# Sums of four rows of q, k and v for the late head pairs: one VectorE instruction each in place of two GpSimd additions

## The chip, the cores and the metric

The kernel runs on one core of a Trainium2 chip. Five engines have instruction queues of their own and work through them in order: TensorE (PE, its weight loads shown apart as PEld), VectorE (DVE), ScalarE (ACT), GpSimd (POOL) and SyncE (SP), which here issues all DMAs. Semaphores order them against each other. The metric is the device time of one execution in microseconds (us); lower is better.

## The reference

Attention for 8 batches and 8 heads, sequence 576, head size 64, in two parts that are added: a global attention on q, k and v averaged over groups of four rows, and a local one with a band of seven keys. A feed-forward network follows.

```python
def _attn_ref(q, k, v):
    q_d = q.reshape(B, H, Sd, factor, D).mean(axis=3)      # factor = 4
    k_d = k.reshape(B, H, Sd, factor, D).mean(axis=3)
    v_d = v.reshape(B, H, Sd, factor, D).mean(axis=3)
    out_up = np.repeat(sm_attn(q_d, k_d, v_d), factor, axis=2)
    mask = np.abs(pos[:, None] - pos[None, :]) < factor
    ...
    return (out_up + out_local).astype(np.float32)

def _moe_ref(x, U, V, w_ch1, w_ch2):
    xt = x.transpose(0, 2, 1)
    h = xt @ U @ V
    u = x + h.transpose(0, 2, 1)
    ch = np.maximum(u @ w_ch1, 0.0) @ w_ch2
    return (u + ch).astype(np.float32)
```

## The kernel before

**Attention** goes by pairs of heads, 32 in all, four to a batch. The four pairs of batch 0 are "early" (`early_global`, `local_blocks`, `early_mix`); the 28 others are "late" and go through `late_global` (L515), `local_attn` (L817) and `mix_part` (L899).

A late pair loads q and k transposed (tiles `gq` and `gT`, 128 partitions, L587) and, for each head, v as `vr` (72 partitions, L528). `pool_halves` (L437) sums each four neighbours of `gq` and of `gT` on GpSimd in two additions: L440 makes `gh`, L442 makes `smq` or `smk`. The v sums are two GpSimd additions for each head: L530 in place, L532 into `vs`. TensorE then makes the scores (`ps_b`, L783 and L790), later transposes the exponentials (`ps_t`, L555) and multiplies by `vs` (`ps_a`, L569). The tiles `gq`, `gT`, `gh` and `vr` have one buffer each, so the next load into one waits until its readers are done.

The local part of a pair keeps GpSimd busy with five products `Pt` (L852), which VectorE reduces (L857), and with `xL` (L923). The mix makes `ps_hu` (L931), `stk` (ScalarE L935 and L939, VectorE L936), `ps_u` (L739), the sum `xT` (VectorE L743), and from it `uH` (ScalarE L746) and `uL` (GpSimd L748), the input of the network.

**The network** runs over 13 tiles of columns (four of 288, nine of 384) times 16 slices of the weights: 208 steps. A step is twelve matmuls into a PSUM tile `ps_h` (`ffn1`, L956), which ScalarE reads into `hH` (L964) and VectorE into `hL` (L965), and three steps later twelve matmuls into `acc` (`ffn2`, L981). Up to step 19 only one bank serves `ps_h`, since the conversion of the weights uses the other; from then on two banks alternate (L950). Tiles 0 and 1 hold batch 0. Tiles 2 and 3 hold batch 1, so step 33 can't run before the four late pairs of batch 1 are through the mix. This point is called the gate below.

**The weights** are loaded (`wr`) and converted during the first steps: ScalarE L347, VectorE L350 and L352, ScalarE L358, GpSimd L362.

**The order** of each engine's queue is made ahead of the run by a planner (`Plan`, L55): every operation has an engine, an estimated duration, a priority, and its dependencies; the planner runs the whole program by these estimates, and an engine that is free takes the ready operation of the best priority. `dve(n, ...)` puts an operation of n elements on VectorE, `pool_tt(n, ...)` on GpSimd. A different engine or duration for a few operations thus orders all queues anew.

Of the kernel before, what the change touches and what calls it, by code (L numbers as in the profile page):

```python
# [11 lines left out]
F32 = mybir.dt.float32  # L12
# [7 lines left out]
ALU = mybir.AluOpType  # L20
AX = mybir.AxisListType
# [33 lines left out]
class Plan:  # L55
# [6 lines left out]
    def buf(self, pool, shape, dt, name, tag=None, bufs=1):  # L62
        return Buf(self, pool, shape, dt, name, tag or name, bufs)

    def op(self, eng, dur, fn, r=(), w=(), prio=0.0, after=(), lat=None, move=0.0, at=0.0, hold=0.0):
        o = Op()
        o.eng, o.dur, o.fn, o.prio, o.succ, o.ndep, o.ready = eng, dur, fn, prio, [], 0, at
        o.lat, o.move = LATENCY[eng] + SLACK * (SLACK_FROM <= prio < 1000) if lat is None else lat, move
        deps = set(after)
        deps.update(d for k in (*r, *w) for d in getattr(getattr(k[0] if isinstance(k, tuple) else k, "pool", None), "gate", ()))  # L70
        bufs = []
        for k in r:
            b = k[0] if isinstance(k, tuple) else k
# [130 lines left out]
def attn_mix_ffn_kernel(ctx: ExitStack, tc, q, kp, vp, qT, kT, v, U, Ub, V, w1, w2, band, eye, pool, vw, ident, outT):  # L204
    nc = tc.nc
    B, H, S, D = q.shape
    HP = H // 2
    NPOS = 9
    SPAD = kp.shape[2]
    SD = S // 4  # L210
# [38 lines left out]
    op, buf = plan.op, plan.buf  # L249
# [23 lines left out]
    def dve(n, fn, r, w, prio, two_x=False, after=()):  # L273
        return op(DVE, ((n / 2 if two_x else n) + 65) / 960.0, fn, r, w, prio, after)
# [4 lines left out]
    def pool_tt(n, fn, r, w, prio, ns=2.11, after=()):  # L279
        return op(POOL, 0.147 + n * ns / 1000.0, fn, r, w, prio, after)  # L280
# [8 lines left out]
    early_pool = early.__enter__()  # L289
# [11 lines left out]
    loc, glo, mix = (Late(n) for n in ("loc", "glo", "mix"))  # L301
# [129 lines left out]
    def work(is_early, pool, shape, dt, name, tag=None, bufs=1):  # L431
        if is_early:
            return buf(early_pool, shape, dt, name, tag, 1 if name == 'gh' else 2)
        return buf(pool, shape, dt, name, tag, bufs)

    heads = [slice(hh * D, (hh + 1) * D) for hh in range(2)]
    def pool_halves(raw, lo, out, e, prio):  # L437
        gh = work(e, glo, [128, SD, 2], F32, "gh")
        x4 = lambda: raw()[:, lo:lo + S].rearrange("p (j r) -> p j r", r=4)
        pool_tt(2 * SD, lambda: nc.gpsimd.tensor_tensor(  # L440
            out=gh(), in0=x4()[..., 0:2], in1=x4()[..., 2:4], op=ALU.add), [raw], [gh], prio, 1.65)
        pool_tt(SD, lambda: nc.gpsimd.tensor_tensor(  # L442
            out=out()[:, 0:SD], in0=gh()[..., 0], in1=gh()[..., 1], op=ALU.add), [gh], [out], prio, 1.75)

    def early_global(b, hp, prio, qt, kt):
        sq = ring([SD + 16], "smq_e")
        sk = work(True, glo, [128, SD], F32, "smk")
        pool_halves(qt, 0, sq, True, prio)
        pool_halves(kt, (SPAD - S) // 2, sk, True, prio)
        od = buf(early_pool, [128, NQ, D], F32, "od_e", None, NOD)  # L450
        vs = buf(early_pool, [QH, 4 * D], F32, "vs_e", None, 2)
        x = (buf(early_pool, [QH, 2, 2, 4, D], F32, "vr") if b else
             buf(wts, [QH, 2, 2, 4, D], F32, "vr", f"W2_{NFC - 6 - hp}:vr"))
        for hh in range(2):
            dma(lambda hh=hh: nc.sync.dma_start(
                out=x()[:, hh], in_=v[b, 2 * hp + hh].rearrange("(a p r) d -> p a r d", a=2, r=4)), [], [(x, hh)], prio, 150)
        pool_tt(512, lambda: nc.gpsimd.tensor_tensor(
            out=x()[:, :, :, 0:2, :], in0=x()[:, :, :, 0:2, :], in1=x()[:, :, :, 2:4, :], op=ALU.add),
            [(x, 0), (x, 1)], [(x, 0), (x, 1)], prio)
        pool_tt(256, lambda: nc.gpsimd.tensor_tensor(  # L460
            out=vs()[:QH].rearrange("p (a h d) -> p h a d", a=2, h=2), in0=x()[:, :, :, 0, :], in1=x()[:, :, :, 1, :],
            op=ALU.add), [(x, 0), (x, 1)], [vs], prio)
# [7 lines left out]
        def s_mm():  # L470
# [8 lines left out]
            out=mx(), in_=pooled_view(ps), axis=AX.X, op=ALU.max), [ps], [mx], prio)  # L479
# [20 lines left out]
        out = lambda: pa()[:, :NQ * D].rearrange("p (a d) -> p a d", a=NQ)  # L500

        def a_mm():
# [8 lines left out]
            out=od()[:NP], in0=out()[:NP], in1=ri()[:NP].unsqueeze(2).broadcast_to([NP, NQ, D]), op=ALU.mult),  # L511
# [3 lines left out]
    def late_global(b, hp, up_s, prio):  # L515
        h0 = 2 * hp
        g = lambda shape, name, bufs=1: buf(glo, shape, F32, name, None, bufs)
        sq, sk = queries[0], g([128, SD], "smk")
        qr, kr = g([128, S], "gq"), g([128, SPAD], "gT")
        load_t(qr, qT, b, h0, prio)  # L520
        load_t(kr, kT, b, h0, prio)
        pool_halves(qr, 0, sq, False, prio)
        pool_halves(kr, (SPAD - S) // 2, sk, False, prio)
        vss = []
        for hh in range(2):
            x, vs = g([QH, 2, 4, D], "vr"), g([QH, 2, D], "vs", 2)
            vss.append(vs)
            dma(lambda hh=hh, x=x: nc.sync.dma_start(  # L528
                out=x(), in_=v[b, h0 + hh].rearrange("(a p r) d -> p a r d", a=2, r=4)), [], [x], prio, 150)
            pool_tt(256, lambda x=x: nc.gpsimd.tensor_tensor(  # L530
                out=x()[:, :, 0:2, :], in0=x()[:, :, 0:2, :], in1=x()[:, :, 2:4, :], op=ALU.add), [x], [x], prio)
            pool_tt(128, lambda x=x, vs=vs: nc.gpsimd.tensor_tensor(  # L532
                out=vs(), in0=x()[:, :, 0, :], in1=x()[:, :, 1, :], op=ALU.add), [x], [vs], prio)
        s_s = buf(dram, [2, S, KL + 1], F32, "s_s", bufs=4)
        ps = late_scores(qr, kr, sq, sk, s_s, prio - 0.4)
        rs, rr, ri, mx, nb = (g([128, NQ], n) for n in ("rs", "rr", "ri", "mx", "nb"))
# [4 lines left out]
            out=mx(), in_=pooled_view(ps), axis=AX.X, op=ALU.max), [ps], [mx], prio)  # L541
# [20 lines left out]
        out = lambda: pa()[:, :NQ * D].rearrange("p (a d) -> p a d", a=NQ)  # L562

        def a_mm():
# [9 lines left out]
            out=od()[:NP], in0=out()[:NP], in1=ri()[:NP].unsqueeze(2).broadcast_to([NP, NQ, D]), op=ALU.mult),  # L574
# [11 lines left out]
    def load_t(t, src, b, h0, prio):  # L586
        dma(lambda: nc.sync.dma_start(out=t(), in_=src[b, h0:h0 + 2].rearrange("h d s -> (h d) s")),  # L587
            [], [t], prio)
# [274 lines left out]
    for g0 in (*range(0, NB * S, TN), *range(NB * S, B * S, TW)):  # L863
        n = TN if g0 < NB * S else TW
        for b in range(g0 // S, (g0 + n - 1) // S + 1):
            lo, hi = max(g0, b * S), min(g0 + n, (b + 1) * S)
# [237 lines left out]
```

## Time and profile before

| what | value |
|---|---|
| median of 3 runs | 1010.79 us (1009.43 to 1011.28) |
| the profiled execution's own time | 1003.93 us |
| its span, first to last instruction | 1002.2 us |
| mean granted TensorE clock in it | 0.986 |
| first of the late sums on GpSimd | 68.2 us after the start |
| last of them (L530) | 750.0 us after the start |

In the profile, a group row gives the line, the engine, the operation, the tiles (written<-read), the shapes, the count, then the busy time in us and the mean of one in ns, and last the engine's idle time just before these instructions with what ended it. A window row gives the busy time of each engine in one stretch of the span, the granted clock (1.00 is full), the share of the DMA engines, and GB/s. A timeline row gives start, duration, and in brackets the idle time before it with its releaser. A row of waits gives total, times, and the longest in us.

### The profile page before, as it was taken

The numbers are of one execution on the slowest core, as the hardware profiler recorded it, in microseconds if no ns is written. First come the engines' busy times: TensorE is split into PE (matmuls) and PEld (weight loads), VectorE is DVE, ScalarE is ACT, GpSimd is POOL, SyncE is SP. The second block draws the span as 40 slices with busy tenths as digits, with TensorE's granted clock in tenths as the row PEclk, the third lists the DMA queues.
The fourth block names the chain that finished last, engine by engine and source line by source line (L and its number), as shares of the span: only waits on it lengthen the run. The fifth ranks groups of instructions, "written<-read, shape, count | busy, mean of one in ns | idle before, by whom it ended". The sixth has DMA issues, their size and how long they took to land.

```text
span 1002.2 us, 24561 instructions
## 1 busy us (share of the span) xinstructions
PE 976.2 (97%) x9896; PEld 942.6 (94%) x9896; DVE 438.3 (44%) x814; ACT 347.1 (35%) x1012; POOL 571.7 (57%) x640
## 2 busy tenths in 40 slices
PE   6979999999999999999999999999999999999998
PEld 4669999899999999999999999999999999999998
DVE  4776664645544454544543544434445222211211
ACT  4866533433333333333433333423422122111110
POOL 6786887986757587657846756844866212300100
PEclk9969999999999999999999999999999999999999
DMA  9958768665554565547545456355462121000000
GB/s 265 317 186 210 205 154 155 154 162 137 131 121 111 130 167 130 132 105 179 144 116 128 102 137 144 83 127 113 113 150 72 32 56 24 32 2 1 32 1 32
DMA packets 220906, 120.04 MB, mean 120 GB/s; under 512 B 174052, under 2 KB 196920, under 8 KB 220792
## 3 DMA queue, kind: packets, MB, share of 16 engines
q1 hardware_dynamic: 220792, 118.47, 47.7%
q8 instruction: 78, 1.28, 0.6%
q14 instruction: 36, 0.29, 0.1%
HBM read 87.57 MB, written 30.86 MB: 118 GB/s over the span
## 4 chain that ended last, share of the span: by engine, by line
PE 86%; DMA 2%; POOL 1%; DVE 1%; ACT 1%; SPq 1%; issue 0%; DVEq 0%; ACTq 0%
PE ps_h L956 38%; PE acc L981 38%; PE ps_a L569 2%; PE ps_b L790 2%; DMA wr<-in_W 2%; PE ps_b L783 2%; PE ps_t L555 2%; PE ps_hu L931 2%; POOL Pt L852 1%; PE ps_u L739 1%; DMA vr<-in_v 1%; SPq L806 1%; DVE acc L857 0%; ACT half L347 0%; ACT E L544 0%
## 5 line engine op out<-in xcount | busy, mean ns | idle before, releaser
L981 PE MATMUL acc<-hH,W 128*128 128x384 f32 (+1 forms) x1664 | 442.3, 327 | 0.0
L956 PE MATMUL ps_h<-uH,W 128*128 128x384 f32 (+1 forms) x1376 | 360.4, 323 | 3.9 <-DVE hL L965 2.9
L981 PEld LDWEIGHTS acc<-hH,W 128*128 128x128 f32 x1664 | 297.3, 188 | 2.4
L981 PE MATMUL acc<-hL,W 128*128 128x384 f32 (+1 forms) x832 | 268.0, 322 | 0.0
L852 POOL TENSOR_TENSOR Pt<-vl,ms 128x896 f32<-128x896 f32 (+1 forms) x140 | 239.6, 1790 | 28.4 <-DMA vl<-in_vp 14.0
L956 PEld LDWEIGHTS ps_h<-uH,W 128*128 128x128 f32 x1376 | 246.3, 190 | 5.7 <-DVE hL L965 3.5
L965 DVE SCALAR_TENSOR_TENSOR hL<-ps_h,hH 128x384 fp32r<-128x384 f32 (+1 forms) x208 | 108.9, 524 | 324.1 <-ACT hH L964 323.8
L964 ACT ACTIVATE hH<-ps_h 128x384 fp32r<-128x384 f32 (+1 forms) x208 | 97.3, 468 | 366.8 <-PE ps_h L956 358.9
L956 PE MATMUL ps_h<-uL,W 128*128 128x384 f32 (+1 forms) x688 | 221.7, 322 | 1.1 <-POOL uL L748 1.1
L857 DVE TENSOR_REDUCE acc<-Pt 128x128 f32<-128x1024 f32 (+1 forms) x140 | 152.8, 1108 | 62.3 <-ACT Pt L846 27.1
L981 PEld LDWEIGHTS acc<-hL,W 128*128 128x128 f32 x832 | 156.7, 188 | 0.0
L956 PEld LDWEIGHTS ps_h<-uL,W 128*128 128x128 f32 x688 | 130.6, 190 | 1.7 <-POOL uL L748 1.7
L956 PE MATMUL ps_h<-u,W 128*128 128x384 f32 x432 | 98.1, 334 | 0.0
L923 POOL TENSOR_TENSOR xL<-xL,xH 116x640 fp32r<-116x640 f32 x28 | 43.9, 1567 | 73.4 <-ACT xH L922 66.8
L846 ACT ACTIVATE Pt<-ul 128x128 f32<-128x128 f32 (+1 forms) x140 | 56.6, 433 | 81.7 <-DVE acc L857 54.9
L991 POOL TENSOR_TENSOR o<-uH,uL 128x384 f32<-128x384 f32 (+1 forms) x43 | 39.0, 940 | 70.0 <-DMA out_t<-o 70.0
L956 PEld LDWEIGHTS ps_h<-u,W 128*128 128x128 f32 x432 | 76.9, 188 | 0.0
L748 POOL TENSOR_TENSOR uL<-xT,uH 128x384 fp32r<-128x384 f32 (+2 forms) x52 | 41.0, 808 | 56.7 <-ACT uH L746 56.7
L530 POOL TENSOR_TENSOR vr<-vr 72x256 f32<-72x256 f32 x56 | 41.2, 736 | 52.4 <-DMA vr<-in_v 51.7
L362 POOL TENSOR_TENSOR W<-c,W 128x512 fp32r<-128x512 f32 x32 | 41.0, 1289 | 14.3 <-ACT W L358 14.3
L743 DVE TENSOR_TENSOR xT<-ps_u,xT 128x384 f32<-128x384 f32 (+2 forms) x64 | 27.4, 452 | 37.2 <-PE ps_u L739 37.1
L790 PE MATMUL ps_b<-smk,smq 64*32 64x144 f32 x672 | 38.9, 296 | 0.0
(133 smaller groups left out, 897.2 us busy)
## 6 DMA issues: line engine op xcount, KB each, us to landing
wr<-in_W SPq DMA_DIRECT2D x32, 511.8 KB
vl<-in_vp SPq DMA_DIRECT2D x56, 240.0 KB
vr<-in_v SPq DMA_DIRECT2D x64, 144.0 KB
gT<-in_kT SPq DMA_DIRECT2D x28, 291.0 KB
gq<-in_qT SPq DMA_DIRECT2D x28, 288.0 KB
up_s<-od SPq DMA_DIRECT2D x168, 48.0 KB
ul<-up_s SPq DMA_DIRECT2D x28, 288.0 KB
x_s<-acc SPq DMA_DIRECT2D x28, 288.0 KB
```

Source lines behind the costliest of these rows:

```text
L362: pool_tt(1.0 * n, lambda: nc.gpsimd.tensor_tensor(out=lo_out(), in0=ta()[l0:], in1=hi_out()[l0:].bitcast(F32), op=ALU.subtract), [t, *own ...
L530: pool_tt(256, lambda x=x: nc.gpsimd.tensor_tensor(out=x()[:, :, 0:2, :], in0=x()[:, :, 0:2, :], in1=x()[:, :, 2:4, :], op=ALU.add), [x], ...
L748: pool_tt(n, lambda uH=uH, uL=uL, uf=uf, us=us: nc.gpsimd.tensor_tensor(out=uL.ap(hp, us), in0=uf(), in1=uH.ap(hp, us).bitcast(F32), op=AL ...
L790: nc.tensor.matmul(pg()[m:m + QL, a * SD:(a + 1) * SD], sq()[o, n:n + QL], sk()[o], start=True, stop=True)
L846: act(n * D, lambda n=n, ps=ps, Pt=Pt: nc.scalar.activation(Pt()[:, :n, :, 7], ul()[:, ps, :], AF.Copy), [ul], [(Pt, 1)], prio, 0.16)
L852: nc.gpsimd.tensor_tensor(out=Pt()[:, :n, :, 0:7].rearrange("p s d o -> p o s d"), in0=win, in1=at()[:, ps, :].rearrange("p s o -> p o s") ...
L857: dve(8.5 * n * D, lambda n=n, ps=ps, Pt=Pt: nc.vector.tensor_reduce(out=acc()[:, ps, :], in_=Pt()[:, :n], axis=AX.X, op=ALU.add), [(Pt, 0 ...
L923: pool_tt(640, lambda: nc.gpsimd.tensor_tensor(out=xL(), in0=xL().bitcast(F32), in1=xH().bitcast(F32), op=ALU.subtract), [xL, xH], [xL], prio)
L956: nc.tensor.matmul(ps()[:, :tn], W1[fc]()[:, w, dc, :], u.ap(dc), start=(n == 0), stop=(n == 3 * NDC - 1))
L964: last_h[i] = act(tn, lambda: nc.scalar.activation(hH()[:, :tn], ps()[:, :tn], AF.Relu), [ps], [hH], FIRST, 0.05)
L965: dve(tn, lambda: nc.vector.scalar_tensor_tensor(hL()[:, :tn], ps()[:, :tn], 0.0, hH()[:, :tn].bitcast(F32), op0=ALU.max, op1=ALU.subtract ...
L981: nc.tensor.matmul(ac[e]()[:, :tn], W2[fc]()[:, w, es], hx()[:, :tn], start=(fc == 0 and n == 0), stop=(fc == NFC - 1 and n == 2))
```

## The change

The late pairs get `pool_late`: one VectorE `tensor_reduce` over groups of four for `smq`, one for `smk`, and one for each head's `vs`, which reads the four rows of v that stand 64 elements apart. The eight GpSimd additions of a late pair and its buffer `gh` go. The early pairs keep `pool_halves`.

```diff
+    def pool_late(raw, lo, out, prio):
+        dve(S, lambda: nc.vector.tensor_reduce(
+            out=out()[:, 0:SD], in_=raw()[:, lo:lo + S].rearrange("p (j r) -> p j r", r=4), axis=AX.X, op=ALU.add),
+            [raw], [out], prio)
+
-    def pool_halves(raw, lo, out, e, prio):
-        gh = work(e, glo, [128, SD, 2], F32, "gh")
+    def pool_halves(raw, lo, out, prio):
+        gh = work(True, early_pool, [128, SD, 2], F32, "gh")
...
-        pool_halves(qr, 0, sq, False, prio)
-        pool_halves(kr, (SPAD - S) // 2, sk, False, prio)
+        pool_late(qr, 0, sq, prio)
+        pool_late(kr, (SPAD - S) // 2, sk, prio)
...
-            pool_tt(256, lambda x=x: nc.gpsimd.tensor_tensor(
-                out=x()[:, :, 0:2, :], in0=x()[:, :, 0:2, :], in1=x()[:, :, 2:4, :], op=ALU.add), [x], [x], prio)
-            pool_tt(128, lambda x=x, vs=vs: nc.gpsimd.tensor_tensor(
-                out=vs(), in0=x()[:, :, 0, :], in1=x()[:, :, 1, :], op=ALU.add), [x], [vs], prio)
+            dve(512, lambda x=x, vs=vs: nc.vector.tensor_reduce(
+                out=vs(), in_=x().rearrange("p a r d -> p a d r"), axis=AX.X, op=ALU.add), [x], [vs], prio)
```

From L438 on, lines of the changed kernel stand three to five numbers higher: L965 becomes L968, L748 becomes L751, L852 becomes L855, L835 becomes L838.

VectorE's queue around the first `hL` of the network, before (`y_h`, `c` and `cu` belong to the conversion of weights, `Ust` to that of U):

```order
L352 SCALAR_TENSOR_TENSOR cu<-ur,y_h 116x160
L350 TENSOR_SCALAR y_h<-half 128x512
L366 SCALAR_TENSOR_TENSOR Ust<-cu,Ust 116x5x32
L352 SCALAR_TENSOR_TENSOR c_1267<-wr,y_h 128x512
L965 SCALAR_TENSOR_TENSOR hL<-ps_h,hH 128x288
```

The same place in the changed kernel:

```order
L352 SCALAR_TENSOR_TENSOR cu<-ur,y_h 116x160
L350 TENSOR_SCALAR y_h<-half 128x512
L438 TENSOR_REDUCE smq<-gq 128x144
L438 TENSOR_REDUCE smk<-gT 128x144
L968 SCALAR_TENSOR_TENSOR hL<-ps_h,hH 128x288
L535 TENSOR_REDUCE vs<-vr 72x128
L366 SCALAR_TENSOR_TENSOR Ust<-cu,Ust 116x5x32
L352 SCALAR_TENSOR_TENSOR c_1267<-wr,y_h 128x512
```

The sums of the first late pair stand ahead of the first `hL`, and two operations of the conversion have moved behind it.

VectorE's queue between the 13th and the 15th `hL`, before (`lsm` and `lrl` belong to the local softmax, `mx` to the global one):

```order
L965 SCALAR_TENSOR_TENSOR hL<-ps_h,hH 128x288
L352 SCALAR_TENSOR_TENSOR c_2043<-wr,y_h 128x512
L965 SCALAR_TENSOR_TENSOR hL<-ps_h,hH 128x288
L831 TENSOR_REDUCE lsm<-ms 128x9
L540 TENSOR_REDUCE mx<-ps_b 128x3
L833 RECIPROCAL lrl<-lse 128x9
L965 SCALAR_TENSOR_TENSOR hL<-ps_h,hH 128x288
```

And in the changed kernel:

```order
L968 SCALAR_TENSOR_TENSOR hL<-ps_h,hH 128x288
L350 TENSOR_SCALAR y_h<-half 128x512
L552 RECIPROCAL ri<-rr 128x3
L834 TENSOR_REDUCE lsm<-ms 128x9
L352 SCALAR_TENSOR_TENSOR c_2168<-wr,y_h 128x512
L968 SCALAR_TENSOR_TENSOR hL<-ps_h,hH 128x288
L535 TENSOR_REDUCE vs<-vr 72x128
L836 RECIPROCAL lrl<-lse 128x9
L438 TENSOR_REDUCE smq<-gq 128x144
L968 SCALAR_TENSOR_TENSOR hL<-ps_h,hH 128x288
```

A sum of v, which waits for a load, and a sum of q, which waits for another, stand between two `hL`, the second of them directly ahead of one.

GpSimd's queue ahead of the gate, before, from the last `xL` of batch 1 to its `uL`:

```order
L923 TENSOR_TENSOR xL<-xL,xH 116x640
L852 TENSOR_TENSOR Pt<-vl,ms 128x7x128 x2
L852 TENSOR_TENSOR Pt<-vl,ms 128x7x64
L826 TENSOR_TENSOR ms<-sc,lmx 128x63
L440 TENSOR_TENSOR gh<-gq 128x288
L530 TENSOR_TENSOR vr<-vr 72x2x128
L442 TENSOR_TENSOR smq<-gh 128x144
L532 TENSOR_TENSOR vs<-vr 72x128
L748 TENSOR_TENSOR uL<-xT,uH 128x288 x2
L835 TENSOR_TENSOR ms<-ms,lrl 128x63
```

In the changed kernel:

```order
L926 TENSOR_TENSOR xL<-xL,xH 116x640
L829 TENSOR_TENSOR ms<-sc,lmx 128x63
L838 TENSOR_TENSOR ms<-ms,lrl 128x63
L855 TENSOR_TENSOR Pt<-vl,ms 128x7x128 x2
L751 TENSOR_TENSOR uL<-xT,uH 128x288 x2
L926 TENSOR_TENSOR xL<-xL,xH 116x640
```

The four sums and one `Pt` are gone from in front of `uL`, and the second `ms`, which waits for VectorE's `lrl`, with two whole `Pt` behind it, now stands ahead of `uL`, where before it stood behind. On TensorE the transposes `ps_t` of a later pair (L558) now stand between `ps_u` and the gate's first `ps_h`; before, none did. On VectorE the last operations ahead of the gate's `stk` are now the fourth read of `acc` (L997), `ri` (L552) and `lrl` (L836).

More of the change, by code (lines that the diff above doesn't have):

```diff
@@ L447, in early_global @@
         sk = work(True, glo, [128, SD], F32, "smk")
-        pool_halves(qt, 0, sq, True, prio)
-        pool_halves(kt, (SPAD - S) // 2, sk, True, prio)
+        pool_halves(qt, 0, sq, prio)
+        pool_halves(kt, (SPAD - S) // 2, sk, prio)
         od = buf(early_pool, [128, NQ, D], F32, "od_e", None, NOD)
```

## The prediction

> **What bounds the kernel now.** I read the page's totals first, then the windows, then the group rows that price the change.
>
> ```profile
> span 1002.2 us, 24561 instructions
> PE 976.2 (97%) x9896; PEld 942.6 (94%) x9896; DVE 438.3 (44%) x814; ACT 347.1 (35%) x1012; POOL 571.7 (57%) x640
> PE 86%; DMA 2%; POOL 1%; DVE 1%; ACT 1%; SPq 1%; issue 0%; DVEq 0%; ACTq 0%
> ```
>
> TensorE is busy 97% of the span, and the chain that ended last runs through it for 86%. GpSimd, from which work is taken, holds 1% of the chain. So GpSimd's time matters only where TensorE waits, and the windows show where that is:
>
> ```profile
> 68.90:139.50 70.60, 68.41 (x805) 66.20 (x806) 44.62 (x82) 37.90 (x99) 56.97 (x66) 0.97 0.75 199
> 150.00:200.00 50.00, 48.45 (x602) 47.03 (x600) 27.68 (x53) 20.90 (x66) 42.73 (x48) 1.00 0.72 154
> 200.00:250.00 50.00, 48.38 (x651) 46.50 (x650) 25.18 (x49) 18.35 (x61) 37.21 (x41) 0.97 0.63 148
> 250.00:300.00 50.00, 50.00 (x509) 49.24 (x508) 23.75 (x45) 18.77 (x57) 32.57 (x39) 1.00 0.56 128
> 550.00:600.00 50.00, 49.31 (x421) 47.57 (x420) 24.21 (x43) 16.48 (x50) 33.62 (x39) 1.00 0.52 118
> ```
>
> The columns behind the stretch are the busy times of PE, PEld, DVE, ACT and POOL. From 250 us on TensorE hardly stops (50.00 of 50); 550 to 600 lacks 0.69. Idle TensorE under the late pairs is 2.2 us in the first 19 steps (68.9 to 139.5), 1.55 and 1.62 on both sides of the gate near 200, and the clock dips there (0.97 of 50 us, 1.5 us). All that GpSimd could give back is some 7 us, and most of it has other causes too.
>
> **What goes from GpSimd.**
>
> ```profile
> L530 POOL TENSOR_TENSOR vr<-vr 72x256 f32<-72x256 f32 x56 | 41.2, 736 | 52.4 <-DMA vr<-in_v 51.7 <-PE ps_h L956 0.7
> L532 POOL TENSOR_TENSOR vs<-vr 72x128 f32<-72x128 f32 x56 | 25.8, 460 | 1.6
> L440 POOL TENSOR_TENSOR gh<-gq 128x288 f32<-128x288 f32 x28 | 18.9, 675 | 12.2 <-DMA gq<-in_qT 12.2
> L440 POOL TENSOR_TENSOR gh<-gT 128x288 f32<-128x288 f32 x28 | 18.7, 669 | 7.0 <-DMA gT<-in_kT 5.6
> L442 POOL TENSOR_TENSOR smk<-gh 128x144 f32<-128x144 f32 x32 | 13.7, 427 | 1.5
> L442 POOL TENSOR_TENSOR smq<-gh 128x144 f32<-128x144 f32 x28 | 11.9, 426 | 1.6
> ```
>
> A late pair loses 0.675 + 0.669 + 0.427 + 0.426 + 2 x (0.736 + 0.460) = 4.59 us; 28 pairs 128.5 us, GpSimd falls from 572 to 443.
>
> **What comes to VectorE.** No row has a sum over groups of four, so I go by the nearest reductions, and for the stride by the nearest pair of strided and dense rows:
>
> ```profile
> L857 DVE TENSOR_REDUCE acc<-Pt 128x128 f32<-128x1024 f32 x112 | 134.8, 1216 | 60.7 <-ACT Pt L846 27.1 <-POOL Pt L852 25.1 <-issue 4.4
> L857 DVE TENSOR_REDUCE acc<-Pt 128x64 f32<-128x512 f32 x28 | 18.9, 674 | 1.6 <-POOL Pt L852 1.5
> L846 ACT ACTIVATE Pt<-ul 128x128 f32<-128x128 f32 x112 | 47.2, 458 | 59.7 <-DVE acc L857 33.0 <-DMA ul<-up_s 25.6 <-POOL xL L923 0.8
> L846 ACT ACTIVATE Pt<-ul 128x64 f32<-128x64 f32 x28 | 9.3, 333 | 22.0 <-DVE acc L857 21.9
> L746 ACT ACTIVATE uH<-xT 128x384 fp32r<-128x384 f32 x18 | 8.6, 518 | 9.9 <-PE ps_h L956 9.6 <-DVE xT L743 0.4
> L746 ACT ACTIVATE uH<-xT 128x192 fp32r<-128x192 f32 x18 | 6.0, 358 | 7.6 <-PE ps_h L956 3.2 <-DVE xT L743 3.2 <-POOL o L991 1.3
> ```
>
> From 1216 and 674 ns a reduction costs (1216 - 674)/512 = 1.06 ns for each element read and 132 ns besides: 0.742 us for 576 dense elements of q or k, 0.674 us for 512. But v is read in steps of 64 elements. ScalarE's strided write (L846, steps of 8 elements) costs (458 - 333)/64 = 1.95 ns an element, its dense one (L746) (518 - 358)/192 = 0.83. If VectorE's strided read pays the same 1.12 ns on top, a sum of v takes 0.674 + 512 x 0.00112 = 1.25 us. I take 1.25, the one strided row of a streaming engine that I have, and keep 0.674 as the other end. VectorE gains 28 x 2 x 0.742 + 56 x 1.25 = 111.5 us (79 at the low end), from 438 to 550 or 518. That still fits the span.
>
> The Trainium skill ("SBUF — State Buffer", section "Door 1: The DMA port swizzle") says that full bandwidth needs consecutive accesses to hit the same 16-byte line, and that every crossing to a new line pays. Steps of 64 fp32 cross each time, so by it the sums of v cost 70 us rather than 38; it gives no factor.
>
> **Term 1, the first 19 steps: +3.8 us.** Here one `ps_h` bank serves, so the next step's twelve matmuls wait for `hL`.
>
> ```profile
> L965 DVE SCALAR_TENSOR_TENSOR hL<-ps_h,hH 128x288 fp32r<-128x288 f32 x64 | 29.0, 453 | 45.9 <-ACT hH L964 45.7
> L964 ACT ACTIVATE hH<-ps_h 128x288 fp32r<-128x288 f32 x64 | 26.3, 411 | 58.8 <-PE ps_h L956 58.5
> 138.77 1.58 PE acc L981 x12
> ```
>
> The cover is the 1.58 us of `acc` matmuls; `hH` and `hL` use 0.41 + 0.45 of it, so 0.72 is left. The new order puts 15 sums between the 1st and the 19th `hL`, eight of q and k and seven of v: 10.7 to 14.7 us more in a stretch where VectorE works 44.6 of 70.6, so 78% to 84% busy. All may fit its 26 us of idle time (0 lost), or each may push TensorE by its length (14.7). Item by item: two sums of v and two of q or k stand directly ahead of an `hL`; beyond the cover that is 2 x (1.25 - 0.72) + 2 x 0.02 = 1.1. And VectorE takes over the waits for the loads:
>
> ```profile
> POOL vr L530 <- DMA vr<-in_v: 2.5, 2, 1.5
> POOL gh L440 <- DMA gq<-in_qT: 1.6, 1, 1.6
> ```
>
> These rows are of GpSimd's waits in 68.9:139.5; three waits of 4.1 us less three covers leave 2.0. That makes 3.1. By scaling instead: the 2.2 us lost now, at a ratio of VectorE's busy to idle time of 44.6/26.0 = 1.7, would grow to 6.7 at 59.3/11.3 = 5.2, so +4.5. I take 3.8, between the two.
>
> **Term 2, the gate: -0.7 us.** The timelines of GpSimd and TensorE there, a group row of VectorE, and a row of the chain:
>
> ```profile
> 181.37 3.89 POOL L852 TENSOR_TENSOR Pt<-vl,ms 128x896 f32<-128x896 f32 x2 [0.39 <-DMA vl<-in_vp]
> 201.37 1.55 POOL L748 TENSOR_TENSOR uL<-xT,uH 128x288 fp32r<-128x288 f32 x2
> 202.88 0.29 POOL L835 TENSOR_TENSOR ms<-ms,lrl 128x63 f32<-128x63 f32 x1
> 196.19 0.46 PE L931 MATMUL ps_hu<-xH,Ust 116*64 116x128 f32 x5
> 198.50 0.50 PE L739 MATMUL ps_u<-Vst,stk 128*128 128x288 f32 x2 [1.55 <-DVE stk L936]
> 201.22 0.40 PE L956 MATMUL ps_h<-uH,W 128*128 128x288 f32 x1 [1.03 <-ACT uH L746]
> 202.21 0.41 PE L956 MATMUL ps_h<-uL,W 128*128 128x288 f32 x1 [0.59 <-POOL uL L748]
> L994 DVE SCALAR_TENSOR_TENSOR o<-acc,o 128x288 f32<-128x288 f32 x16 | 6.5, 454 | 0.3 <-PE acc L981 0.2
> 625.71 0.66 PE ps_t L555 x6
> ```
>
> TensorE waits 1.55 + 1.03 + 0.59 = 3.2 us here, and `uL` lets it go 6.0 us after `ps_hu` began (196.19 to 202.2). In the new order the four sums and a `Pt` are out of the way, but two whole `Pt` (3.89) and a `ms` that waits for VectorE's `lrl` stand ahead of `uL`. `lrl` comes behind the last read of `acc`, which ends with the matmuls just ahead of `ps_hu`; I put it 0.9 us behind the start of `ps_hu` (that read, 0.45, and two short reciprocals; an estimate). Then 0.3 for `ms`, 3.9 for `Pt`, 0.8 (half of 1.55) for the first `uL`: 5.9 us, as late as now. What improves is that the transposes of a later pair (0.66) fill part of the wait. Ends: all of 3.2 and the dip of 1.5 gained (-4.7), or `lrl` 2 us later (+1.5).
>
> **Term 3, the stop in 550 to 600: -0.7 us.** Its chain went through a `vr` load that waited for the GpSimd sum of the head before. One VectorE instruction frees `vr` sooner; at most the 0.69 goes.
>
> **Term 4, waits for loads from step 20 on: +1.1 us.**
>
> ```profile
> POOL vr L530 <- DMA vr<-in_v: 51.7, 21, 9.7
> POOL gh L440 <- DMA gq<-in_qT: 12.2, 7, 3.3
> POOL gh L440 <- DMA gT<-in_kT: 5.6, 3, 2.4
> L965 DVE SCALAR_TENSOR_TENSOR hL<-ps_h,hH 128x384 fp32r<-128x384 f32 x144 | 79.9, 555 | 278.2 <-ACT hH L964 278.1
> L964 ACT ACTIVATE hH<-ps_h 128x384 fp32r<-128x384 f32 x144 | 70.9, 493 | 308.0 <-PE ps_h L956 300.4 <-PE ps_u L739 7.4
> 640.02 2.08 PE ps_h L956 x12
> ```
>
> These 69.5 us move to VectorE, and `hL` queues behind. With two banks the cover is three groups of twelve matmuls, 3 x 2.08 = 6.2, less `hH` 0.49 and `hL` 0.56: 5.2 us. Of 31 waits one, of 9.7, is longer, and would cost 4.5. Between 0 and 4.5, or more if such waits multiply, I take a quarter.
>
> Sum: 3.8 - 0.7 - 0.7 + 1.1 = +3.5 on the profiled execution's 1003.93 us, so 1007.4. The three timed runs lie higher (median 1010.79); the same 3.5 on it gives 1014.3.
>
> **Rivals.** *The relief wins, faster*: VectorE's 26 us of idle time hide the sums in the early steps (term 1 zero), no long wait lands on it (term 4 zero), and `uL` runs ahead of the two `Pt` in effect, because `lrl` comes before `acc` ends. Then 3.2 at the gate and 0.7 in 550 to 600 go: 1006.9, and 1005.4 with the clock dip gone too. For it speaks GpSimd's 42.73 of 50 us ahead of the gate; against it, that `uH` and `stk`, of other engines, ended most of the gate's wait. It decides whether the stretch to step 19 keeps its 2.2 us of idle TensorE. The Trainium skill ("GPSIMD Engine Reference", section "4.1 Engine selection") sends elementwise work and reductions along the free dimension to VectorE, GpSimd being about half as fast; taken as a rule for this kernel it means this case. Here 4.59 us a pair become 2.83 to 3.98 by the rows above, so the trace agrees on the work, not on what TensorE waits for.
>
> *Hidden anyway, no change*: the losses fit the cover and the gate stays as it is: 1010.8. For it speaks 50.00 of 50 in the stretch from 250 us.
>
> *Long waits on VectorE, much slower*: with loads issued in a new order, two more waits like that of 9.7 us stand ahead of an `hL`: 3.5 + 2 x 4.5 = +12.5, 1023. It needs waits beyond 5.2 us; before there was one.
>
> **How the numbers follow.** Forecast case 0.45 (from +1 to +8; 0.38 slower, 0.07 the same), relief 0.23 (0.20 faster, 0.03 the same), hidden 0.20, long waits 0.12. About 0.2%, 2 us, is what a measurement of this kernel can tell from no change. Faster 0.20, same 0.30, slower 0.50. The range from 1006 to 1022 leaves out the end of the relief case with the dip gone (0.06) and the worse half of the long waits (0.06), and holds both prices of a sum of v. The likeliest case's own range is 1011.8 to 1019.
>
> **What would show it.** The sums of q and k as VectorE rows near 0.74 us, those of v near 1.25 rather than 0.67; GpSimd at 443 us. Term 1: TensorE's idle time from the first to the 19th `hL` near 6 us, with waits of `ps_h` for `hL`. Term 2: waits of about 2.5 us at the gate, the last ended by `uL`. Term 4: VectorE waits for `gq`, `gT` and `vr`, few beyond 5 us. I am wrong if the early steps lose nothing, if the gate opens before GpSimd's two `Pt` are done, or if TensorE stops after 250 us.

## The result and the profile after

The changed kernel takes 1016.79 us (median of 9 runs, 1012.54 to 1020.71), the kernel before 1010.79 us in the same session (9 runs, 1008.22 to 1012.53). The ratio is 1.0071, 95% interval 1.0049 to 1.0092: slower by 0.7%. The profiled execution took 1016.65 us.

The totals and the chain on the page of the changed kernel:

```profile
span 1014.9 us, 24387 instructions
PE 977.7 (96%) x9896; PEld 941.9 (93%) x9896; DVE 520.9 (51%) x926; ACT 344.6 (34%) x1012; POOL 454.9 (45%) x416
PE 68%; DMA 8%; DVE 7%; SPq 4%; POOL 3%; issue 2%; ACT 2%; DVEq 0%; ACTq 0%; POOLq 0%
```

GpSimd has lost 117 us of work and VectorE has gained 83. TensorE does the same 9896 matmuls, but the chain that ended last now runs through it for 68% instead of 86%; DMA and VectorE hold 15% of it, 3% before. So work now ends late on other engines. The windows show where. The first row of the next fence runs from the first `hL` to the 19th, the stretch of the prediction's first row; the others are single stretches of 50 us and all that lies behind 250 us. The columns are as before (PE, PEld, DVE, ACT, POOL, granted clock, DMA share, GB/s):

```profile
72.60:143.50 70.90, 70.21 (x902) 67.77 (x903) 57.59 (x103) 39.32 (x110) 43.55 (x36) 0.95 0.85 215
200.00:250.00 50.00, 46.02 (x557) 43.64 (x556) 30.89 (x58) 18.12 (x59) 26.35 (x22) 1.00 0.66 156
400.00:450.00 50.00, 47.76 (x501) 45.89 (x500) 31.81 (x53) 16.96 (x52) 31.08 (x26) 1.00 0.58 133
500.00:550.00 50.00, 47.97 (x489) 46.05 (x495) 33.61 (x54) 16.42 (x53) 24.28 (x20) 0.97 0.62 151
550.00:600.00 50.00, 48.47 (x588) 46.02 (x589) 31.53 (x53) 19.77 (x65) 27.66 (x26) 1.00 0.64 153
250.00:1014.90 764.90, 753.67 (x6648) 736.61 (x6646) 345.94 (x597) 216.15 (x639) 297.46 (x258) 1.00 0.40 93
```

The first 19 steps, where the prediction put most of the loss, lost nothing: TensorE is idle for 70.90 - 70.21 = 0.7 us (2.2 before) although VectorE is busy for 81% of that stretch. Just ahead of it one of the sums does stop TensorE, for 1.88 us:

```profile
72.86 0.46 PE L793 MATMUL ps_b<-smk,smq 64*32 64x144 f32 x4 [1.88 <-DVE smk L438]
```

But from the first step of the network to the 19th `hL`, that stop included, TensorE is idle for 4.0 us where it was 4.5 before. And the 33rd `hL`, the first behind the gate, starts 140.1 us after the first step in both profiles. So up to the gate nothing was lost. From 250 us to the end TensorE is idle for 11.2 us. The kernel before, in the same view:

```profile
250.00:1002.20 752.20, 747.79 (x6628) 732.96 (x6626) 287.73 (x519) 218.66 (x640) 378.03 (x413) 1.00 0.40 95
```

There it was 4.4. In both, 3.7 us of this lie behind TensorE's last matmul, so that the stops are 7.5 us after and 0.7 before. The difference, 6.8 us, is made of single stops in a stretch that hardly had any.

The two profiled executions are 12.7 us apart, the medians 6.0. Part of that is not the change: the first step of the network starts at 63.2 us in the profile of before and at 67.0 in that of after, while the queues up to there differ in nothing. From the first step on the two profiles differ by 8.8 us. The profile of before is also that of a short execution, 1003.93 us, where the nine timed ones begin at 1008.22. So the two profiles show more loss than the medians do.

**One of the new stops.** Timeline rows of ScalarE, VectorE and TensorE of the changed kernel, out of the stretch from 538 us on:

```profile
538.32 0.45 ACT L849 ACTIVATE Pt<-ul 128x128 f32<-128x128 f32 x1 [5.08 <-DMA ul<-up_s]
...
538.85 1.22 DVE L860 TENSOR_REDUCE acc<-Pt 128x128 f32<-128x1024 f32 x1 [7.26 <-ACT Pt L849]
...
540.45 1.21 DVE L860 TENSOR_REDUCE acc<-Pt 128x128 f32<-128x1024 f32 x1
541.58 1.07 DVE L535 TENSOR_REDUCE vs<-vr 72x128 f32<-72x512 f32 x1
...
542.70 1.09 PE L572 MATMUL ps_a<-vs,E 72*48 72x64 f32 x22 [2.03 <-DVE vs L535]
```

Read it from the bottom. TensorE stops for 2.03 us because `ps_a` needs a sum of v. The sum stands in VectorE's queue behind the local reductions `acc` of another pair. The first of these had VectorE stand idle for 7.26 us, since ScalarE's `Pt` waited 5.08 us for `ul`, which had to come back from DRAM. A load that lands late thus stops TensorE through whatever stands behind it in an in-order queue.

**The prices.** Group rows of VectorE after, with its waits for the loads of the sums:

```profile
L535 DVE TENSOR_REDUCE vs<-vr 72x128 f32<-72x512 f32 x56 | 60.9, 1087 | 28.7 <-DMA vr<-in_v 28.6
L438 DVE TENSOR_REDUCE smk<-gT 128x144 f32<-128x576 f32 x28 | 20.8, 743 | 8.7 <-DMA gT<-in_kT 8.7
L438 DVE TENSOR_REDUCE smq<-gq 128x144 f32<-128x576 f32 x28 | 20.7, 738 | 13.5 <-DMA gq<-in_qT 13.4
L860 DVE TENSOR_REDUCE acc<-Pt 128x64 f32<-128x512 f32 x28 | 18.8, 673 | 2.3 <-POOL Pt L855 1.8 <-ACT Pt L849 0.3
```

A sum of q or k takes 0.74 us, as worked out. A sum of v takes 1.087 us, between the two ends of 0.674 and 1.25; the last row, as many elements without the stride, takes 0.673, so the stride of 64 elements costs (1087 - 673)/512 = 0.81 ns an element. (A v sum also writes 128 results where that row writes 64. The sums of q and k write 144 and still cost what the dense rows gave, so the number of results isn't what costs.) VectorE waits 28.6 + 8.7 + 13.4 = 50.7 us for the loads of the sums.

### The profile page after: what moved, and what is told of

Same layout as the page of the kernel before. It is cut to its first block, busy times and chain, and to the rows that moved or that the text cites. A ratio compares the mean times of both kernels' runs of the same rounds, so it can differ in the third digit from the quotient of the medians.

```text
span 1014.9 us, 24387 instructions
## 1 busy us (share of the span) xinstructions
PE 977.7 (96%) x9896; PEld 941.9 (93%) x9896; DVE 520.9 (51%) x926; ACT 344.6 (34%) x1012; POOL 454.9 (45%) x416
## 4 chain that ended last, share of the span: by engine, by line
PE 68%; DMA 8%; DVE 7%; SPq 4%; POOL 3%; issue 2%; ACT 2%; DVEq 0%; ACTq 0%; POOLq 0%
PE acc L984 30%; PE ps_h L959 30%; DVE acc L860 3%; DMA ul<-up_s 3%; POOL Pt L855 2%; SPq L582 2%; PE ps_a L572 2%; DMA vr<-in_v 1%; PE ps_b L793 1%; DMA wr<-in_W 1%; PE ps_hu L934 1%; PE ps_b L786 1%; PE ps_t L558 1%; SPq L809 1%; DMA x_s<-acc 1%
## 5 line engine op out<-in xcount | busy, mean ns | idle before, releaser
L855 POOL TENSOR_TENSOR Pt<-vl,ms 128x896 f32<-128x896 f32 (+1 forms) x140 | 241.4, 1790 | 96.0 <-DVE acc L860 69.1
L968 DVE SCALAR_TENSOR_TENSOR hL<-ps_h,hH 128x384 fp32r<-128x384 f32 (+1 forms) x208 | 108.5, 521 | 289.4 <-ACT hH L967 289.0
L751 POOL TENSOR_TENSOR uL<-xT,uH 128x384 fp32r<-128x384 f32 (+2 forms) x52 | 40.9, 808 | 112.1 <-ACT uH L749 111.8
L926 POOL TENSOR_TENSOR xL<-xL,xH 116x640 fp32r<-116x640 f32 x28 | 43.9, 1566 | 72.7 <-ACT xH L925 46.6
L535 DVE TENSOR_REDUCE vs<-vr 72x128 f32<-72x512 f32 x56 | 60.9, 1087 | 28.7 <-DMA vr<-in_v 28.6
L786 PE MATMUL ps_b<-gT,gq 64*32 64x38 f32 x2016 | 37.0, 201 | 0.0
```

The costliest lines, as they stand in the source:

```text
L535: dve(512, lambda x=x, vs=vs: nc.vector.tensor_reduce(out=vs(), in_=x().rearrange("p a r d -> p a d r"), axis=AX.X, op=ALU.add), [x], [vs] ...
L751: pool_tt(n, lambda uH=uH, uL=uL, uf=uf, us=us: nc.gpsimd.tensor_tensor(out=uL.ap(hp, us), in0=uf(), in1=uH.ap(hp, us).bitcast(F32), op=AL ...
L786: nc.tensor.matmul(pl()[m:m + QL, x:x + KL], qr()[o, n * QL:(n + 1) * QL], kr()[o, n * QL:n * QL + KL], start=True, stop=True)
L855: nc.gpsimd.tensor_tensor(out=Pt()[:, :n, :, 0:7].rearrange("p s d o -> p o s d"), in0=win, in1=at()[:, ps, :].rearrange("p s o -> p o s") ...
L926: pool_tt(640, lambda: nc.gpsimd.tensor_tensor(out=xL(), in0=xL().bitcast(F32), in1=xH().bitcast(F32), op=ALU.subtract), [xL, xH], [xL], prio)
L968: dve(tn, lambda: nc.vector.scalar_tensor_tensor(hL()[:, :tn], ps()[:, :tn], 0.0, hH()[:, :tn].bitcast(F32), op0=ALU.max, op1=ALU.subtract ...
```

## The experiments

Every kernel was timed 6 to 12 times beside the kernel before on the same chip. Ratios are to it; below 1 is faster. "Order" is the order of the engines' queues that the planner makes; "told" is a figure that the planner takes for an operation.

### Engine and order taken apart

The change does two things: it puts the sums on VectorE, and since the planner now takes GpSimd for freer, it orders all queues anew. Each was done without the other.

**The order before, sums on VectorE.** The planner still counts the additions on GpSimd; what is issued at the place of the second is the VectorE sum (v alike):

```diff
+            pool_tt(2 * SD, lambda: None, [raw], [gh], prio, 1.65)
+            pool_tt(SD, lambda: nc.vector.tensor_reduce(
+                out=out()[:, 0:SD], in_=raw()[:, lo:lo + S].rearrange("p (j r) -> p j r", r=4), axis=AX.X, op=ALU.add),
+                [gh, raw], [out], prio, 1.75)
```

> All queues stand as in the kernel before, but each late sum is one VectorE instruction, at the place in time that the plan gave to the second addition on GpSimd. If the loss is VectorE's own: ratio 1.005 to 1.015, since here the plan does not even know of the work on VectorE. If it is the new order: 0.998 to 1.003.

Measured: 1008.76 us, ratio 0.999 (0.997 to 1.001). In the order before, the full work of the sums on VectorE costs nothing. The traces show that order kept: all other operations of VectorE, ScalarE, GpSimd and SyncE follow each other as in the kernel before, one for one.

```profile
250.00:1009.00 759.00, 753.38 (x6753) 737.99 (x6751) 351.07 (x601) 219.69 (x643) 300.22 (x259) 1.00 0.40 95
L537 DVE TENSOR_REDUCE vs<-vr 72x128 f32<-72x512 f32 x56 | 59.7, 1065 | 9.1 <-DMA vr<-in_v 9.0
```

In this kernel's window row TensorE is idle for 5.6 us from 250 us on, near the 4.4 of before, with VectorE as busy (351) as in the changed kernel (346). Its group row has the same price for a sum of v, but VectorE waits 9.0 us for `vr`, not 28.6.

**The new order, sums on GpSimd.** The queues of the changed kernel, with the two GpSimd additions issued where VectorE's sum was planned:

```diff
-        dve(S, lambda: nc.vector.tensor_reduce(
...
+        def adds():
...
+            nc.gpsimd.tensor_tensor(out=gh()[:], in0=x4()[..., 0:2], in1=x4()[..., 2:4], op=ALU.add)
+            nc.gpsimd.tensor_tensor(out=out()[:, 0:SD], in0=gh()[..., 0], in1=gh()[..., 1], op=ALU.add)
+        dve(S, adds, [raw], [out], prio)
```

> All queues stand as in the changed kernel, but the late sums are issued to GpSimd as two additions each, at the places that the plan gave to VectorE. If the loss is VectorE's own (sums that stand in its queue behind other waits, with TensorE waiting for the sum or for hL): ratio to before 0.998 to 1.003, stops of TensorE between 250 and 650 us under 3 us in all, against 7.5 in the changed kernel. If the loss is the new order of the other engines: ratio 1.005 to 1.010 again, with the same 7 us of stops.

Measured: 1038.68 us, ratio 1.029 (1.0261 to 1.0319), outside both expectations. An order made for a freer GpSimd costs 2.9% when GpSimd isn't freer. So the sums do load GpSimd there; but the test says nothing on whether the order is good for the engine it was made for.

### One half of the change at a time

```diff
 # sums of q and k on VectorE, those of v back on GpSimd
-            dve(512, lambda x=x, vs=vs: nc.vector.tensor_reduce(
+            pool_tt(256, lambda x=x: nc.gpsimd.tensor_tensor(
...
+            pool_tt(128, lambda x=x, vs=vs: nc.gpsimd.tensor_tensor(
```

> Only the sums of q and k go to VectorE, 41 us of work, waits for gq and gT with them. If the longer sums of v (1.09 us each where the plan has 0.60) and the waits for vr carry the loss: ratio 0.998 to 1.003. If any sum on VectorE costs alike: about 1.0035, half of the change. A new order of its own may add or take 2 us.

Measured: 1014.71 us, ratio 1.0049 (1.0028 to 1.0071). And the other half, the kernel before with the sums of v alone on VectorE:

> Only the sums of v go to VectorE, 61 us of work with waits for vr. If the sums of v carry the loss: ratio 1.005 to 1.010. If any sum on VectorE costs alike: about 1.0035. A new order of its own may add or take 2 us.

Measured: 1007.30 us, ratio 0.9973 (0.9955 to 0.999), below both expectations for it and faster than both kernels. The half with the expensive, strided instruction gains, the half with the cheap one loses. By the price of the instructions it should be the other way round; in both halves, too, the planner ordered all queues anew.

### What in the new order costs?

In the changed kernel the last late pair's weighted sum `ps_a` stands at step 134 of 208, before at 152: the planner packs the pairs closer. First guess: that is too close. Second: the plan has a v sum at 0.60 us where it takes 1.09. Third: there is no single cause, any new order moves the time by some tenths of a per cent. Four kernels for these.

**Old pace.** Each late pair's sums of q and k are held back in the plan to the place they have before:

```diff
+PACE = (66.2, 78.6, 92.6, 128.8, ...
-        pool_late(qr, 0, sq, prio)
+        at = PACE[b * HP + h0 // 2 - NE]
+        pool_late(qr, 0, sq, prio, at)
```

> The changed kernel, with each late pair's two sums of q and k held back in the plan to the place where the kernel before has them, so that the late pairs come at the old pace (the last pair's weighted sum at step 150 of 208; before 152, changed kernel 134). Nothing else is edited. Theory 'packing' (the new order brings the late pairs' work closer together, and TensorE then stops for it): ratio 0.997 to 1.002, no stop over 1 us between 250 and 600 us. Theory 'false duration' (the plan takes a v sum for 0.60 us where it takes 1.09, so that what it puts behind the sums comes too early): as the changed kernel, 1.005 to 1.009. Theory 'luck of the draw' (any new order moves the time by some tenths of a per cent, to either side, with no single cause): anywhere from 0.995 to 1.010.

Measured: 1014.87 us, ratio 1.0033 (1.0013 to 1.0053). The old pace brings back about half of the loss (the two intervals just meet), less than "packing" asked for. One half of the change had spoken against packing already: with v alone the last weighted sum stands at step 139, and that kernel is faster than the kernel before. The kernel with the lowest ratio, further below, has it at step 132.

**True durations.** The plan is told 1.09 us for a v sum, then 0.745 us for q and k as well (so far 0.67, by the formula in `dve`, not the 0.60 of the expectation, which is that of a v sum):

```diff
-            dve(512, lambda x=x, vs=vs: nc.vector.tensor_reduce(
+            dve(978, lambda x=x, vs=vs: nc.vector.tensor_reduce(
...
-        dve(S, lambda: nc.vector.tensor_reduce(
+        dve(650, lambda: nc.vector.tensor_reduce(
```

> The changed kernel, with the plan told 1.09 us for a v sum in place of 0.60 us, which is what the trace shows; the instructions are the same, their order is planned anew (last weighted sum at step 135, the changed kernel has 134). 'False duration': 0.997 to 1.002. 'Packing': as the changed kernel, 1.005 to 1.009. 'Luck of the draw': anywhere from 0.995 to 1.010.

> As the kernel that is told 1.09 us for a v sum, and told 0.745 us for a sum of q or k too (0.60 before; the trace shows 0.74). Last weighted sum at step 136. 'False duration': 0.997 to 1.002, and no slower than with v's duration alone. 'Packing': 1.005 to 1.009. 'Luck of the draw': anywhere from 0.995 to 1.010, and up to 0.5% from the kernel told of v alone.

Measured: 1017.01 us, ratio 1.0056 (1.0035 to 1.0077), and 1022.98 us, ratio 1.0102 (1.0068 to 1.0136). True durations don't help; "false duration" falls.

**The kernel before, nudged.** Nothing is moved; one figure of the plan changes by 4%:

```diff
-                out=x()[:, :, 0:2, :], in0=x()[:, :, 0:2, :], in1=x()[:, :, 2:4, :], op=ALU.add), [x], [x], prio)
+                out=x()[:, :, 0:2, :], in0=x()[:, :, 0:2, :], in1=x()[:, :, 2:4, :], op=ALU.add), [x], [x], prio, 2.0)
```

> The kernel before, all sums on GpSimd, with one figure of its plan nudged: the first addition of v is told as 0.66 us in place of 0.69 us. The plan then comes out in another order (last weighted sum at step 149; 152 before), with the same instructions and nothing relieved. 'Packing' and 'false duration': 0.998 to 1.002, since pace and engines are as before. 'Luck of the draw': over 0.2% from 1 in either direction, which would mean that a part of the changed kernel's 0.7% needs no cause beyond a new order.

Measured: 1021.62 us, ratio 1.0112 (1.0086 to 1.0137). This kernel has the instructions of the kernel before on the same engines, and loses more than the changed kernel does. Three windows of it:

```profile
150.00:200.00 50.00, 48.82 (x580) 47.04 (x579) 22.19 (x43) 19.06 (x65) 34.75 (x40) 1.00 0.68 140
200.00:250.00 50.00, 43.03 (x510) 41.32 (x509) 24.02 (x45) 16.54 (x50) 35.64 (x38) 0.90 0.53 123
250.00:1025.20 775.20, 766.04 (x6840) 749.76 (x6838) 296.11 (x537) 224.51 (x664) 392.48 (x427) 1.00 0.41 96
```

TensorE is idle for 1.2 + 7.0 = 8.2 us of the 100 around the gate (3.2 before, on both sides of 200 us), with the clock at 0.90 in the second half on top (0.97 before), and for 9.2 us from 250 us on (4.4 before). A change of 0.03 us in one planned figure made those stops. A loss of 0.7% after a change that replans everything therefore needs no cause in what the change moves.

### Late loads, and three more plans

The stop at 540 us began with a transfer for which ScalarE, and VectorE behind it, stood. That it landed later than the plan had it is inferred; no run shows the plan's own times. To test it, the plan was told that every transfer of the pairs from batch 2 on lands 0.75 us later, in the changed kernel and, as its control, in the kernel before:

```diff
-        late = (1.5 if r else 2.0) * (50 <= prio < 80) + 0.75 * (prio >= 80)
+        late = (1.5 if r else 2.0) * (50 <= prio < 80) + 1.5 * (prio >= 80)
```

> The changed kernel, with the plan told that the loads of the late pairs land 0.75 us later than it took so far. Theory 'late loads' (a new order loses where a load lands after its planned time and VectorE stands for it in front of work that TensorE needs): 0.996 to 1.002, and less idle time of TensorE after 250 us than the changed kernel's 11.2 us. 'Luck of the draw' with no such cause: anywhere from 1.002 to 1.011.

> The kernel before with the same edit: loads of the late pairs planned to land 0.75 us later. 'Late loads': 0.994 to 1.000. 'Luck of the draw', and the order before is a lucky one: 1.002 to 1.011.

Measured: the changed kernel 1006.45 us, ratio 0.9967 (0.9952 to 0.9982); the kernel before 1008.70 us, ratio 0.9984 (0.9968 to 1.0001). With all late sums on VectorE this is the lowest ratio measured here (that of v alone, 0.9973, can't be told from it), and by the medians of two sessions 10.3 us below the changed kernel. Its window and group rows (`smq` shows no wait):

```profile
250.00:1004.50 754.50, 750.32 (x6730) 734.63 (x6729) 347.69 (x598) 215.73 (x643) 298.29 (x258) 1.00 0.41 94
L535 DVE TENSOR_REDUCE vs<-vr 72x128 f32<-72x512 f32 x56 | 60.7, 1084 | 13.5 <-DMA vr<-in_v 13.3
L438 DVE TENSOR_REDUCE smk<-gT 128x144 f32<-128x576 f32 x28 | 20.8, 742 | 6.1 <-DMA gT<-in_kT 5.9
L438 DVE TENSOR_REDUCE smq<-gq 128x144 f32<-128x576 f32 x28 | 20.7, 738 | 0.0
```

TensorE is idle for 4.2 us from 250 us on, where the changed kernel has 11.2, at the same work on VectorE (348 and 346 us). VectorE's waits for the loads of the sums fall from 50.7 to 13.3 + 5.9 = 19.2 us. In the views of waits of that stretch, TensorE's own rows are these in the changed kernel:

```profile
PE acc L984 <- DVE o L997: 2.5, 2, 1.7
PE ps_a L572 <- DVE vs L535: 2.0, 1, 2.0
PE ps_t L558 <- DVE xT L746: 1.0, 2, 0.6
```

and four of 0.4 to 0.6 us; with later loads told, one is left:

```profile
PE ps_b L793 <- DVE xT L746: 0.4, 1, 0.4
```

**The other nudge.** The kernel before, told 0.736 us for the first addition of v, which is its measured time, in place of 0.69:

> The kernel before, all sums on GpSimd, with the same figure of the plan nudged to the other side: the first addition of v is told as 0.736 us in place of 0.69 us (0.736 is what the trace shows). 'Luck of the draw', and the order before is a lucky one: 1.002 to 1.012. Rival 'the plan told shorter than true is what hurt' (the nudge to 0.66 us lost 1.1% since it was further from the truth): 0.995 to 1.001.

Measured: 1011.47 us, ratio 1.001 (0.9994 to 1.0025). That isn't a loss, so the kernel before is no rare stroke of luck: of its three replanned versions one lost 1.1%, one stayed, one came out 0.16% lower with an interval that reaches 1. It doesn't exclude the rival of the expectation, that a plan told less than the truth is what hurt: 1.001 is the upper end of its range. Against that rival stand the changed kernels told true durations, which lost 0.6% and 1.0%.

**Less work in the sums.** The queues of the changed kernel, each sum replaced by a copy of one of its four rows:

```diff
-        dve(S, lambda: nc.vector.tensor_reduce(
+        dve(S, lambda: nc.vector.tensor_copy(
+            out()[:, 0:SD], raw()[:, lo:lo + S].rearrange("p (j r) -> p j r", r=4)[..., 0]),
```

> The changed kernel with its queues word for word, in which each of the 112 late sums is a copy of one of the four rows (144 or 128 elements in place of 576 or 512; three of the four rows are left out of the sums). Theory 'luck of the draw' (the loss belongs to the order of all the other work): 1.003 to 1.008, the stops of TensorE between 250 and 600 us stay. Rival 'VectorE's time' (the new order is good, and the sums' time on VectorE, 102 us of its 521, makes it late): 0.996 to 1.001.

Measured: 1019.35 us, ratio 1.0095 (1.0071 to 1.0118). The loss stays, but as a test of VectorE's time this is weaker than planned: the copies still took 69.5 of the 102.4 us (the last section shows why).

### All versions side by side

The last two columns come from the profiles: TensorE's idle time from 250 us on, and VectorE's waits for the loads of the late sums.

| kernel | ratio | TensorE idle, us | VectorE waits, us |
|---|---|---|---|
| before | 1 | 4.4 | none |
| before, nudged down | 1.0112 | 9.2 | none |
| before, nudged up | 1.001 | 4.7 | none |
| before, loads told later | 0.9984 | 3.8 | none |
| changed | 1.0071 | 11.2 | 50.7 |
| changed, told v | 1.0056 | 7.3 | 54.2 |
| changed, told all | 1.0102 | 11.1 | 63.1 |
| changed, old pace | 1.0033 | 9.1 | 35.3 |
| changed, loads told later | 0.9967 | 4.2 | 19.2 |
| sums on VectorE in the order before | 0.999 | 5.6 | 10.8 |
| new order, sums on GpSimd | 1.029 | 19.5 | none |
| new order, copies for sums | 1.0095 | 9.5 | 57.2 |
| v alone on VectorE | 0.9973 | 6.1 | 43.9 |
| q and k alone on VectorE | 1.0049 | 6.7 | 31.7 |

Among the six versions with all late sums, whole, on VectorE, the two that wait least for the loads are the two that lose nothing; the four that wait 35 us or more all lose. It isn't the whole rule, since v alone waits 43.9 us and gains. Where the sums are on GpSimd, the waits for the same loads are GpSimd's: 69.5 us before, 83.8 nudged down, 59.0 nudged up and 56.2 with loads told later, so that the loser waits longest here too; but in the new order with sums on GpSimd, the slowest of all, they are 29.9.

The columns compare single executions. Those of "nudged down", "old pace" and "new order, sums on GpSimd" were the longest of their kernels' runs, that of "told v" the shortest. Of each idle time, 3.7 us lie behind TensorE's last matmul.

## Why the prediction was right, and where not

The forecast was 1014.3 us, slower by 3.5; measured are 1016.79 and 6.0. The sign and the range held, but for the most part not by the terms of the sum: the largest, +3.8, came to nothing, and stops priced at +1.1 came to 6.8. That the total came out near is luck. Two of the three signs that the prediction named for being wrong came true: the early steps lose nothing, and TensorE stops after 250 us.

- **What goes and what comes**: right in the prices. GpSimd is at 454.9 us (443 predicted), VectorE at 520.9 (518 to 550), but these totals don't measure the prices: the sums' rows add up to 60.9 + 20.8 + 20.7 = 102.4 us, and VectorE's busy time grew by 83. Rows that follow each other closely overlap in the trace, and busy time counts the overlap once; the prediction added and took off means of rows. The sums of q and k cost 0.74 us as worked out. A sum of v costs 1.087 us; ScalarE's strided write overstated the price of the stride (0.81 ns an element, not 1.12).
- **The Trainium skill's rule on the stride** ("SBUF — State Buffer", section "Door 1: The DMA port swizzle") named the right side: steps beyond a 16-byte line cost something. Here that made the 56 sums of v 23 us longer than dense ones, and by the version in the order before it cost nothing in time.
- **Term 1, +3.8 us in the first 19 steps**: wrong, the step that failed first. TensorE's idle time went from 2.2 to 0.7 us, with VectorE busy for 57.59 of 70.90 us. The sign that it named for being wrong, early steps that lose nothing, is what came. That a sum stands ahead of `hL` was read rightly from the order; that it pushes TensorE by what exceeds the cover was not borne out, and the scaling by VectorE's busy to idle time failed with it. The relief rival's first condition, that VectorE's idle time hides the early sums, so came true; its second, that no long wait lands on VectorE, did not.
- **Term 2, the gate, -0.7 us**: right in mechanism, and in size for the waits at the gate. The rows of TensorE and GpSimd after:

```profile
201.84 0.53 PE L742 MATMUL ps_u<-Vst,stk 128*128 128x288 f32 x2 [1.06 <-DVE stk L939]
202.79 0.89 PE L558 MATMUL ps_t<-ident_sb,E 128*72 128x128 f32 x6 [0.42 <-DVE xT L746]
206.12 0.40 PE L959 MATMUL ps_h<-uL,W 128*128 128x288 f32 x1 [1.13 <-POOL uL L751]
201.36 0.29 POOL L838 TENSOR_TENSOR ms<-ms,lrl 128x63 f32<-128x63 f32 x1 [1.31 <-DVE lrl L836]
201.78 3.63 POOL L855 TENSOR_TENSOR Pt<-vl,ms 128x896 f32<-128x896 f32 x2
205.27 1.55 POOL L751 TENSOR_TENSOR uL<-xT,uH 128x288 fp32r<-128x288 f32 x2
```

  The waits are 1.06 + 0.42 + 1.13 = 2.6 us, 3.2 before. `lrl` lets `ms` go, two `Pt` follow, then `uL`, which ends the last wait 6.1 us after `ps_hu` began (200.01 us; 5.9 predicted), and `ps_t` fills part of it. The stretch as a whole still got no better: from 150 to 250 us TensorE is idle for 4.0 us, 3.2 before, since behind the gate comes a new stop of 1.26 us, for a sum of v (at 216.50 us, `ps_a` for `vs`).
- **Term 3, the stop in 550 to 600, -0.7 us**: wrong. That stretch lacks 1.53 us, 0.69 before. No matmul there waits for a sum of v any more (0.41 us before), but the new order has stops of its own, ended by `o` (0.77 us), `xT` (0.40) and `lmx` (0.35).
- **Term 4, waits from step 20 on, +1.1 us**: the right place, and too small. From 250 us on TensorE lost 6.8 us more than before by the windows. The term counted one long wait ahead of `hL`, a quarter of 4.5 us. Most of the waits that did stop TensorE ended at `o`, `vs` and `xT`; what stood ahead were reductions behind late transfers as much as the sums. The longest stop is the one at 542.70 us shown above; the next begins with `ul` in the same way:

```profile
417.96 0.69 ACT L849 ACTIVATE Pt<-ul 128x128 f32<-128x128 f32 x2 [5.13 <-DMA ul<-up_s]
418.50 2.35 DVE L860 TENSOR_REDUCE acc<-Pt 128x128 f32<-128x1024 f32 x2 [6.88 <-ACT Pt L849]
421.83 0.44 PE L984 MATMUL acc<-hH,W 128*128 128x384 f32 x1 [1.68 <-DVE o L997]
```

  The two make 3.7 of the 7.5 us, and neither begins with a load of the sums. Such a load stands ahead of the stops of 0.77 us at 591.60 (`vs` had waited 2.86 us) and of 0.56 us at 482.19 (`smk` had waited 4.32 us).
- **What the sum left out**: that replanning alone moves the time. The kernel before, nudged in one figure, lost 1.1%; the same sums on VectorE lost nothing in the old order and gained 0.33% in an order with later loads told. The working priced the sums, and none of the prices was what decided.

Shown by runs: the sums on VectorE cost nothing in the order before; the loss belongs to the new order that the planner made; the old pace of the pairs brings back about half of it, which a new order alone could do as well, and the told durations of the sums bring back nothing that can be told from noise. Supported, not shown: that the order loses because its loads land later than planned. That edit did what was expected of it in both kernels, and waits and stops fell with it, but it also draws a new order, and one draw for each kernel can't be told from a lucky one when a nudge of 0.03 us moves 1.1%. Still open: which of the moved operations makes each stop.

## What to carry to other kernels

Where a planner orders the queues, a change of engine or cost is also a new draw of the order: measure the new engine in the old order, and an idle nudge of the old kernel, before giving a loss or a gain below a per cent to the change. When an instruction that waits for a load moves to a busier engine, give that load more room in the plan; here the same sums went from 1.0071 to 0.9967 with it, though one new order by itself could have done that too. Count what stands behind a waiting instruction in its queue, not only the one consumer nearest to it.

## What the runs showed of the hardware beside that

**VectorE's copies wait for GpSimd, its reductions do not.** Group rows of the kernel that copies one row in place of each sum:

```profile
L535 DVE COPY vs<-vr 72x128 f32<-72x128 f32 x56 | 38.8, 692 | 32.2 <-DMA vr<-in_v 32.2
L438 DVE COPY smq<-gq 128x144 f32<-128x144 f32 x28 | 16.0, 572 | 16.1 <-DMA gq<-in_qT 16.0
```

A copy reads a quarter of the elements of a sum, and its mean is still 64% and 78% of the sum's. The mean hides two kinds. Timeline rows of VectorE and GpSimd at two places of this kernel:

```profile
583.95 0.21 DVE L535 COPY vs<-vr 72x128 f32<-72x128 f32 x1
584.32 1.56 POOL L926 TENSOR_TENSOR xL<-xL,xH 116x640 fp32r<-116x640 f32 x1 [2.03 <-ACT xH L925]
...
605.23 3.80 DVE L535 COPY vs<-vr 72x128 f32<-72x128 f32 x1
605.18 3.77 POOL L855 TENSOR_TENSOR Pt<-vl,ms 128x896 f32<-128x896 f32 x2 [1.61 <-DMA vl<-in_vp]
```

At 583.95 us GpSimd is idle and the copy takes 0.21 us. At 605.23 it starts 0.05 us after two `Pt` and ends with them, 3.80 us later. Over all copies of v, those beside an idle GpSimd have a median of 0.21 us, those with GpSimd busy for nine tenths of their time or more 1.16 us (0.22 to 3.80). The sums of v of the changed kernel show nothing of the kind: 1.08 us beside an idle GpSimd, 1.10 us beside a busy one. The Trainium skill ("SBUF — State Buffer", section "Who interferes with whom") says that copies of VectorE can take a port pair shared with GpSimd, as an exclusive lock, and that on this chip `tensor_reduce` never does; these rows agree. So a reduction was the right form for these sums, and the kernel of copies is no clean measure of a lighter VectorE.

**The start varies.** In all fourteen kernels the queues of VectorE, ScalarE, GpSimd and SyncE are the same up to the first step of the network. Yet it starts between 63.2 and 72.2 us in their profiles, and 3.9 us later in that of the changed kernel than in that of before. So a few microseconds between one profile and another say nothing until the stretches from the first step on are compared. From there to the end the profiles take 939.0 us before, 947.8 changed, 940.4 with the sums on VectorE in the order before, and 934.2 with loads told later, in the order of the ratios but for 939.0 and 940.4, whose ratios, 1 and 0.999, can't be told apart.
